# Attention: k and v in five slots with the rest rows, one reduction for k's maximum, the rest rows placed with the pair's second batch

## The chip, the cores and the metric
One Trainium2 chip, one core. The metric is the device time in microseconds (us) of one execution of the whole program: a linear attention over 8 batches and two mixture-of-experts layers behind it, in one launch.

## The reference
Shapes: q, k and v are [8 batches, 8 heads, 576 rows, 64]; x is 4608 tokens of 512; each of the two expert layers has 8 experts of 512 to 1024 to 512.

```
q_s = exp(q - max over d);    q_s /= sum over d
k_s = exp(k - max over rows); k_s /= sum over rows
kv  = k_s^T v                          # per head, 64 x 64
x   = q_s kv                           # to [4608, 512]
layer 1: tokens with x.w_skip > 0: x += gate * (relu(x w1[e]) w2[e]),  e = argmax(x w_gate)
layer 2: out = gate * (relu(x w1[e]) w2[e]),  e = argmax of the cosine of x and expert e, over tau
```

## The kernel before, in words
**Attention.** The 576 rows of a batch don't fill whole tiles of 128 partitions. The first 512 lie in four slots (partition p holds rows 4p to 4p+3, tiles `kt`, `vt`, `qt` of 128 x 8 heads x 4 slots x 64). The last 64, the rest rows, have tiles of their own (`kr`, `vr`, `qr`): the even batch of a pair has partitions 0 to 63 there, the odd batch 64 to 127. For each batch `do_k` finds the maximum of k over all rows, in two halves of four heads: VectorE takes pairwise maxima (L190 over slots 0,1 against 2,3; L191 over the two that are left; L192 with the rest rows, on 64 partitions), TensorE transposes (L194), VectorE reduces (L196), ScalarE spreads (L197), TensorE transposes back (L199), ScalarE copies to `mb` (L201). Then k minus the maximum is formed on GpSimd, in the batches of the parameter `kV` on VectorE (L203 for the slots, L205 or L206 for the rest rows), ScalarE takes the exponential (L207, L209) and copies v beside a column of ones (L208, L210). TensorE multiplies over the four slots (L219) and the rest rows (L220). `do_q` does the like for q (L255 to L262), on GpSimd except for the batches in `qV`. `do_out` transposes (L275), copies (L285), multiplies with kv and the router columns in one product (L290), and VectorE divides out of PSUM: L296, L297, L298 into `xb` (the token rows), L299 into `lp` (the logits by head). The rest rows of a pair go through as a slot of their own, into `xr` and `lr`.

**Placing.** `place` takes the slots of one batch (half a batch for the last two, the parameter `tail`; one slot for the rest rows of a pair: 14 calls in all) and finds each token's experts and its row in the DRAM table X: a sum over heads (L319), some ten small VectorE operations (L320 to L327, L338, L340, L341), three kinds of small products on TensorE (L330 to L332), two small copies on ScalarE (L342, L343), and for each slot one indirect DMA from GpSimd's queue (L348). L321 writes the shifted logits into the token rows in SBUF, L322 reads them there; the other intermediates lie in the SBUF tile `rt`, and the product's ranks in a PSUM tile `pr` from L330 to L340. `pr` is one of the four PSUM tiles `p1`, which the transposes and the products of k and v use too.

**The order.** All steps of attention are tasks with a due time (`step`, `off`, `ob` in `PRM`), a cost for each engine that can take them, and the tiles that they read and write. The planner `Order` makes the order of each engine's queue from these when the kernel is built: at each turn it takes, among the tasks that can start earliest, the one with the lowest due time. The engines run their queues in that order and wait for each other by semaphores. The tiles of a name are few (kt 2, vt 2, qt 2, xb 2, p1 4, po 2), and a task waits until one is free. SyncE issues the loads, in planned order too.

**Behind attention.** When the last `place` has the counts (`accF`), the first expert layer starts: the first 512 tokens of expert 0 are in the tile GE by then (L371, behind the placing of batch 6), its weights in the tiles of k and v (L358). L505 and L506 split weights into two parts on ScalarE, VectorE and GpSimd. Then both layers run in steps of 256 tokens. This code is the same before and after, up to a slice of the ring of token tiles.

Of the kernel before, what the change touches and what calls it, by code (L numbers as in the profile page):

```python
# [94 lines left out]
def attention(tc,nc,raw,ctx,cst,q,k,v,routers,wgt,enD,X,accF,w1,w2,early,prm={}):  # L95
# [68 lines left out]
    def load(t,src,b,prio,n,by):  # L164
        x=val((t+'t',b),t+'t',2); y=val((t+'r',b//2),t+'r',2)
        if t=='k': add(prio-.1,dict(D=.65),lambda e: nc.sync.dma_start(out=y.tile[half(b)],in_=rest(src,b)),writes=[(y,b%2)],lat=1.3,dma=.73)
        elif b%2==(t=='q'):
            add(prio+.1,dict(D=1.24),lambda e: [nc.sync.dma_start(out=y.tile[half(o)],in_=rest(src,b//2*2+o)) for o in range(2)],writes=[y],lat=1.3,dma=1.46)
        for g in range(n):
            def f(e,g=g):  # L170
                if by=='h': a=slice(H//n*g,H//n*g+H//n); nc.sync.dma_start(out=x.tile[:,a],in_=main(src,b)[:,a])
                else: nc.sync.dma_start(out=x.tile,in_=main(src,b))
            add(prio,dict(D=.48),f,writes=[x] if n==1 else [(x,g)],lat=1.25,dma=2.91/n)
        return x,y
    def pt(x,n,g): return [x] if n==1 else [(x,g)]
    def do_k(b):
        i=b//2; h=half(b); t0=b*step; n=fine.get(b,1); u=t0+at('k',b); NH=H//n; NC=4//n
        kt,kr=load('k',k,b,u-5,n,'h'); vt,vr=load('v',v,b,t0+at('v',b)-5,n,'h')
        m1=val(('m1',b),parts=2); m2=val(('m2',b),parts=2); m2b=val(('m2b',b),parts=2); mb=val(('mb',b),parts=2); ek=val(('ek',b),parts=2)
        vp=val(('vp',b),parts=2); vq=val(('vq',i),parts=2)  # L180
        fast=b in prm.get('kV',())

        ke=val(('ke',b),parts=2) if b%2 and not fast else None; kx=ke or kr
        for g in range(n):
            hs=slice(NH*g,NH*g+NH); cs=slice(NC*g,NC*g+NC); w=NC*128
# [11 lines left out]
            add(u+2,dict(A=.43/n+.09),lambda e,cs=cs: A.copy(m2b.tile[:,cs],m2.tile[:,cs].unsqueeze(2).to_broadcast([128,NC,128])),pt(m2,n,g),pt(m2b,n,g))  # L197
# [7 lines left out]
            if ke is None: add(u+3.4,sc,lambda e,hs=hs: E[e].tensor_tensor(out=kr.tile[h,hs],in0=kr.tile[h,hs],in1=mb.tile[h,hs],op=ALU.subtract),pt(mb,n,g),krp)  # L205
            else: add(u+3.4,sc,lambda e,hs=hs: E[e].tensor_tensor(out=ke.tile[:,hs],in0=kr.tile[:,hs],in1=mb.tile[:,hs],op=ALU.subtract),pt(mb,n,g)+[kr],pt(ke,n,g))  # L206
            add(u+4,dict(A=1.73/n+.07),lambda e,hs=hs: A.activation(out=ek.tile[:,:,hs],in_=ek.tile[:,:,hs],func=AF.Exp),[],pt(ek,n,g))  # L207
            add(t0+at('v',b),dict(A=1.73/n+.07),lambda e,hs=hs: A.copy(vp.tile[:,hs,:,0:D],vt.tile[:,hs]),pt(vt,n,g),pt(vp,n,g))  # L208
# [4 lines left out]
        for a in range(2):
            pk=val(('p1','kv',b,a)); ks=val(('ks',b,a)); p3=val(('p1','c',b,a)); p4=val(('p1','d',b,a))
            for c2 in range(2):
                c=2*a+c2
                def f(e,pk=pk,c=c,c2=c2):
                    o=pk.tile[:,130*c2:130*c2+130].rearrange("p (g w) -> p g w",g=2)
                    for j in range(NB): T.matmul(o,lhsT=ek.tile[:,j,2*c:2*c+2].rearrange(hd),rhs=vp.tile[:,2*c:2*c+2,j],start=j==0,stop=False)  # L219
                    T.matmul(o,lhsT=kx.tile[h,2*c:2*c+2].rearrange(hd),rhs=vq.tile[h,2*c:2*c+2],start=False,stop=True)  # L220
# [42 lines left out]
    def do_out(b):  # L263
# [3 lines left out]
        xb=val(('xb',b),parts=NB); lp=val(('lp',b),parts=NB); xr=val(('xr',i)); lr=val(('lr',i))  # L267
        order=list(range(NB+b%2))
        if b%2: order=[NB]+order[:-1]
        for z,j in enumerate(order):  # L270
            w=u+1.5*z; rem=j==NB
# [28 lines left out]
            if rem: place(('r',i),1,[xr],[lr],lambda: xr.tile.unsqueeze(1),lambda: lr.tile.unsqueeze(1),w+4,cst['ids'][:,4*B+i:4*B+i+1])  # L300
        ng=2 if b in tail else 1; NJ=NB//ng
        for g in range(ng):
            js=slice(NJ*g,NJ*g+NJ); parts=range(js.start,js.stop)
            place((b,g),NJ,[(xb,j) for j in parts],[(lp,j) for j in parts],lambda js=js: xb.tile[:,js],lambda js=js: lp.tile[:,js],at('S',b)-off['S']+(u+8 if ng==1 else u+1.5*(order.index(js.stop-1)+1)+1),cst['ids'][:,4*b+js.start:4*b+js.stop])
    units=[]; UE=prm.get('early',B-2)
    for b in range(B):
        if b%2: units.append(('r',b//2))
        units+=[(b,g) for g in range(2 if b in tail else 1)]
    def place(key,nj,xk,lk,xt,lt,prio,ids):
# [7 lines left out]
        def w(a,b): return rt.tile[:,0:nj,a:b]  # L317
# [3 lines left out]
        add(prio,dict(V=c),lambda e: V.tensor_tensor(out=xt()[:,:,512:528].rearrange("p j (g e) -> p j g e",g=2),in0=l2(),in1=w(16,18).unsqueeze(3).to_broadcast([128,nj,2,8]),op=ALU.subtract),[ls,rt],xk)  # L321
# [538 lines left out]
```

## Time and profile before

| | us |
|---|---|
| median of 3 runs | 1089.13 (1087.38 to 1093.6) |
| the profiled execution: device time / span | 1090.26 / 1088.5 |
| TensorE busy | 984.2 (90%) |
| VectorE busy | 632.7 (58%) |
| ScalarE busy | 466.7 (43%) |
| GpSimd busy | 413.9 (38%) |
| mean granted TensorE clock | 0.958 |

The page gives shares over the whole span; attention is its first 206 us. In the rows below PE is TensorE's matmul, PEld its weight load, DVE VectorE, ACT ScalarE, POOL GpSimd, SP SyncE. "<-" names what ended an idle time.

### The profile page before, as it was taken

The page shows a single profiled execution, that of the slowest core. Times are in us where ns is not written, and L with a number is a line of the kernel's source. Part 1 is how long each engine was busy: PE and PEld are TensorE (multiplying, and loading weights), DVE is VectorE, ACT ScalarE, POOL GpSimd, SP SyncE. Part 2 cuts the span into 40 slices and gives each one's busy share as a digit, 9 for nine tenths or more (in the row PEclk, how much of TensorE's full clock was granted, in tenths as well). Part 3 has the DMA queues.
Part 4 walks back from the last instruction along what each step waited for, and adds up shares of the span by engine and source line. Part 5 has one row for each costly group of instructions (what it writes and reads, how often), then busy time and mean ns, then how long its engine had stood idle before and what let it go on. Part 6 is the DMA issues. An engine that isn't in the chain of part 4 may idle for free. (4 is left out here: it accounts for less than half of the span.)

```text
span 1088.5 us, 19924 instructions
## 1 busy us (share of the span) xinstructions
PE 984.2 (90%) x6083; PEld 872.4 (80%) x6083; DVE 632.7 (58%) x1624; ACT 466.7 (43%) x971; POOL 413.9 (38%) x369
## 2 busy tenths in 40 slices
PE   3989689589789999999998899999999999999993
PEld 2868588478578988777997789988898899998892
DVE  4798888777546776675776533244443612265470
ACT  5757456412743326243223532262643531365351
POOL 6547544601793817438221730031221310043140
PEclk9988889789989999999999899999999999999998
DMA  9976543563353522425111156034160620062510
GB/s 282 301 231 216 170 156 119 202 217 121 119 205 102 181 76 82 157 88 196 48 42 44 50 192 232 21 121 146 31 231 21 231 71 21 21 212 82 185 38 22
DMA packets 84412, 143.72 MB, mean 132 GB/s; under 512 B 19215, under 2 KB 43791, under 8 KB 84064
## 3 DMA queue, kind: packets, MB, share of 16 engines
q1 hardware_dynamic: 74304, 114.37, 32.8%
q0 software_dynamic: 8640, 26.61, 6.4%
q8 instruction: 75, 1.23, 0.5%
q14 instruction: 145, 1.19, 0.4%
q10 hardware_dynamic: 1248, 0.32, 0.1%
HBM read 110.03 MB, written 33.68 MB: 132 GB/s over the span
## 5 line engine op out<-in xcount | busy, mean ns | idle before, releaser
L536 PE MATMUL P<-xT,w1h 128*128 128x256 f32 x1856 | 345.4, 288 | 5.1 <-ACTq L722 2.3
L566 PE MATMUL py<-w2h,hT 128*128 128x512 f32 x1072 | 343.6, 396 | 2.7 <-issue 2.4
L536 PEld LDWEIGHTS P<-xT,w1h 128*128 128x128 f32 x1856 | 298.3, 197 | 8.3 <-issue 3.6
L536 PE MATMUL P<-xT,w1l 128*128 128x256 f32 x928 | 267.9, 289 | 9.8 <-DVE w1l L506 5.3
L566 PEld LDWEIGHTS py<-w2h,hT 128*128 128x128 f32 x1072 | 201.6, 189 | 46.6 <-DVE hT L513 3.7
L566 PE MATMUL py<-w2l,hT 128*128 128x512 f32 x536 | 211.3, 394 | 4.4 <-POOL w2l L506 3.3
L540 DVE SCALAR_TENSOR_TENSOR hT<-P,hT 128x512 fp32r<-128x512 f32 x116 | 77.7, 687 | 213.4 <-ACT hT L539 204.3
L536 PEld LDWEIGHTS P<-xT,w1l 128*128 128x128 f32 x928 | 182.3, 196 | 11.6 <-POOL w1l L506 5.5
L638 DVE SCALAR_TENSOR_TENSOR jk<-py,enB 128x512 bf16<-128x512 f32 x198 | 136.9, 691 | 24.3 <-ACT xb L574 10.7
L578 POOL DMA_INDIRECT out_dram<-y,idt x38 | 38.2, 1006 | 287.5 <-ACT y L577 234.0
L539 ACT ACTIVATE hT<-P 128x512 fp32r<-128x512 f32 x116 | 68.0, 596 | 180.4 <-PE P L536 176.0
L566 PEld LDWEIGHTS py<-w2l,hT 128*128 128x128 f32 x536 | 101.2, 189 | 32.9 <-POOL w2l L506 10.3
L506 POOL TENSOR_TENSOR w1l<-kt,w1h 128x512 fp32r<-128x512 f32 x64 | 84.2, 1344 | 59.9 <-ACT w1h L505 51.8
L506 POOL TENSOR_TENSOR w2l<-vt,w2h 128x512 fp32r<-128x512 f32 x76 | 101.8, 1368 | 1.4 <-issue 0.8
L577 ACT ACTIVATE y<-py,gate 128x512 f32<-128x512 f32 x38 | 26.1, 688 | 117.6 <-PE py L566 110.9
L290 PE MATMUL po<-KV,eT 128*128 128x164 f32 x256 | 48.6, 342 | 11.7 <-DVE xr L298 9.0
L505 ACT CAST w2h<-vt 128x512 fp32r<-128x512 f32 x104 | 55.5, 617 | 6.4 <-issue 4.0
L505 ACT CAST w1h<-kt 128x512 fp32r<-128x512 f32 x104 | 55.6, 638 | 0.0
L290 PEld LDWEIGHTS po<-KV,eT 128*128 128x128 f32 x256 | 42.3, 216 | 13.4 <-DVE xr L298 9.5
L574 ACT COPY xb<-py 128x512 f32<-128x512 f32 x17 | 10.0, 587 | 96.9 <-DVE flag L649 50.6
L348 POOL DMA_INDIRECT X<-xb,pi x32 | 33.1, 1035 | 44.1 <-ACT pi L343 35.5
L513 DVE TENSOR_TENSOR hT<-P,hT 128x512 fp32r<-128x512 f32 x18 | 12.4, 687 | 63.8 <-ACT hT L512 63.8
(261 smaller groups left out, 1392.1 us busy)
## 6 DMA issues: line engine op xcount, KB each, us to landing
vt<-in_moe_w_dram SPq DMA_DIRECT2D x26, 1024.0 KB
kt<-in_moe_w_dram SPq DMA_DIRECT2D x26, 1024.0 KB
xb<-X SPq DMA_DIRECT2D x56, 266.0 KB
kt<-in_k_dram SPq DMA_DIRECT2D x16, 512.0 KB
vt<-in_v_dram SPq DMA_DIRECT2D x16, 512.0 KB
qt<-in_q_dram SPq DMA_DIRECT2D x8, 1024.0 KB
xg<-X SPq DMA_DIRECT2D x28, 266.0 KB
X<-empty SPq DMA_DIRECT2D x16, 266.0 KB
```

The source lines that it names most:

```text
L290: T.matmul(po.tile[:,c,0:CW],lhsT=eT.tile[:,c] if g is None else eT.tile[:,g,c],rhs=kv.tile[:,c],start=n==0,stop=n==len(ins)-1)
L348: i=P.indirect_dma_start(out=X,out_offset=IO(pi.tile[:,j:j+1]),in_=xt()[:,j],in_offset=None,bounds_check=ZROW,oob_is_err=False)
L505: nc.scalar.copy(h,a)
L506: (nc.gpsimd if lo[2*f+i]=='P' else nc.vector).tensor_tensor(out=l,in0=a,in1=h.bitcast(F32),op=ALU.subtract)
L513: self.nc.vector.tensor_tensor(out=l,in0=p,in1=h.bitcast(F32),op=ALU.subtract)
L536: T.matmul(o,lhsT=w[:,c,128*f:128*f+128],rhs=x[:,c],start=n==0,stop=n==11); n+=1
L539: A.activation(out=h,in_=q,func=AF.Relu)
L540: V.scalar_tensor_tensor(out=hl[:,f-1:f+1],in0=q,scalar=0.0,in1=h.bitcast(F32),op0=ALU.max,op1=ALU.subtract)
L566: T.matmul(self.py[t],lhsT=x[:,c,a],rhs=w[:,c],start=n==0,stop=n==23); n+=1
L577: A.activation(out=y,in_=p,func=AF.Copy,scale=gt)
L578: P.indirect_dma_start(out=self.out,out_offset=IO(self.idt[:,i:i+1]),in_=y,in_offset=None,bounds_check=NTOK-1,oob_is_err=False)
L638: for e in range(n) if 'V' in eng else (): self.nc.vector.scalar_tensor_tensor(out=self.jk,in0=self.py[t],scalar=1.0,in1=self.enB[:,e],op0 ...
```

## The change
- `kt`, `vt` get a fifth slot for the rest rows, as do `ek` (k's exponentials) and `vp` (v and ones). k's rest rows are loaded twice, into both halves of the partitions, in front of the main load; v's once, into partitions 0 to 63, and the other half of that slot is zero, with zeros in place of the ones. `kr`, `vr`, `vq`, `ke` are gone, with L192, L205, L206, L209, L210 and L220: one operation each now covers five slots, and the product runs over five slots of 128 partitions.
- k's maximum over the slots is one reduction per half (four heads x 64 columns x 5 slots, the slot as the innermost axis, 64 elements apart) in place of L190, L191 and L192.
- In the batches of `kV` the subtraction takes the maximum from PSUM; the copy to `mb` (L201) is left out there.
- The output of an odd batch has five slots in one tile `xb` (the pair's rest rows first). They are placed with that batch: 10 calls of `place` in place of 14. For the last batch the calls have three slots and two.
- In `place` the intermediates lie in the PSUM tile `pr`, which is taken at the first of them; ScalarE copies the shifted logits to the token rows at the end.
- The costs given to the planner and all its due times are new; `kV` is (1,6) for (3,7), `qV` (2,) for (7,), and `nA` (batches whose kv is scaled out of PSUM on ScalarE) (1,2,3,6,7) for (0,2,3,4,6,7).

```diff
-    mk('kt',[128,H,NB,D],nb['kt'],raw); mk('vt',[128,H,NB,D],nb['vt'],raw)
+    mk('kt',[128,H,NS,D],nb['kt'],raw); mk('vt',[128,H,NS,D],nb['vt'],raw)
...
+            add(prio-.1,dict(D=1.1),lambda e: [nc.sync.dma_start(out=x.tile[half(o),:,NB],in_=r) for o in range(2)],writes=[(x,2)],lat=1.3,dma=1.0)
+        else: add(prio-.1,dict(D=.6),lambda e: nc.sync.dma_start(out=x.tile[0:64,:,NB],in_=r),writes=[(x,2)],lat=1.3,dma=.5)
...
-            add(u,dict(V=1.07/n+.06),lambda e,hs=hs,t=t: V.tensor_tensor(out=t(),in0=kt.tile[:,hs,0:2],in1=kt.tile[:,hs,2:4],op=ALU.max),pt(kt,n,g),pt(ek,n,g))
-            add(u,dict(V=.54/n+.06),lambda e,hs=hs,t=t: V.tensor_tensor(out=m1.tile[:,hs],in0=t()[:,:,0],in1=t()[:,:,1],op=ALU.max),pt(ek,n,g),pt(m1,n,g))
-            add(u,dict(V=.54/n+.06),lambda e,hs=hs: V.tensor_tensor(out=m1.tile[h,hs],in0=m1.tile[h,hs],in1=kr.tile[h,hs],op=ALU.max),krp,pt(m1,n,g))
+            add(u,dict(V=1.40),lambda e,hs=hs: V.tensor_reduce(out=m1.tile[:,hs],in_=kt.tile[:,hs].rearrange("p h j d -> p h d j"),axis=AX.X,op=ALU.max),kp,pt(m1,n,g))
...
+            if fast:
+                add(u+3.5,dict(V=1.40),lambda e,hs=hs,p2=p2,w=w: V.tensor_tensor(out=ek.tile[:,:,hs].rearrange("p j h d -> p h j d"),in0=kt.tile[:,hs],in1=p2.tile[:,0:w].rearrange("p (h d) -> p h d",d=D).unsqueeze(2).to_broadcast([128,NH,NS,D]),op=ALU.subtract),kp+[p2],pt(ek,n,g))
...
-                    for j in range(NB): T.matmul(o,lhsT=ek.tile[:,j,2*c:2*c+2].rearrange(hd),rhs=vp.tile[:,2*c:2*c+2,j],start=j==0,stop=False)
-                    T.matmul(o,lhsT=kx.tile[h,2*c:2*c+2].rearrange(hd),rhs=vq.tile[h,2*c:2*c+2],start=False,stop=True)
+                    for j in range(NS): T.matmul(o,lhsT=ek.tile[:,j,2*c:2*c+2].rearrange(hd),rhs=vp.tile[:,2*c:2*c+2,j],start=j==0,stop=j==NB)
...
-            if rem: place(('r',i),1,[xr],[lr],lambda: xr.tile.unsqueeze(1),lambda: lr.tile.unsqueeze(1),w+4,cst['ids'][:,4*B+i:4*B+i+1])
-        ng=2 if b in tail else 1; NJ=NB//ng
+        ng=2 if b in tail else 1; cut=[0,ns] if ng==1 else [0,ns-2,ns]
...
-        def w(a,b): return rt.tile[:,0:nj,a:b]
+        def w(a,b): return pr.tile[:,96:96+36*NS].rearrange("p (j c) -> p j c",c=36)[:,0:nj,a:b]
+        def sh(): return pr.tile[:,288:288+16*NS].rearrange("p (j c) -> p j c",c=16)[:,0:nj]
+        rt=pr
...
-        add(prio,dict(V=c),lambda e: V.tensor_tensor(out=xt()[:,:,512:528].rearrange("p j (g e) -> p j g e",g=2),in0=l2(),in1=w(16,18).unsqueeze(3).to_broadcast([128,nj,2,8]),op=ALU.subtract),[ls,rt],xk)
+        add(prio,dict(V=c),lambda e: V.tensor_tensor(out=sh().rearrange("p j (g e) -> p j g e",g=2),in0=l2(),in1=w(16,18).unsqueeze(3).to_broadcast([128,nj,2,8]),op=ALU.subtract),[ls],[rt])
...
+        add(prio+.3,dict(A=.22),lambda e: A.copy(xt()[:,:,512:528],sh()),[pr],xk)
```

## Rows read from the trace of the kernel before

**Rows 1.** Busy time by stretch: us, then busy us (instructions) by engine, clock, DMA share, GB/s.
```profile
0.00:206.00 206.00, 156.64 (x1015) 138.42 (x1016) 166.35 (x449) 116.81 (x258) 109.85 (x118) 0.90 0.68 208
...
40.00:190.00 150.00, 126.15 (x833) 114.20 (x833) 133.64 (x345) 90.40 (x204) 78.58 (x58) 0.87 0.59 190
...
8.00:40.00 32.00, 22.14 (x127) 17.35 (x127) 20.14 (x34) 20.80 (x40) 18.32 (x14) 1.00 1.15 316
```

**Rows 2.** Timeline of GpSimd, VectorE and TensorE: start, us, engine, line, instruction.
```profile
104.28 9.25 DVE L321 TENSOR_TENSOR xb<-ls,rt 128x64 f32<-128x64 f32 x1
...
108.82 4.63 POOL L203 TENSOR_TENSOR ek<-kt,mb 128x1024 f32<-128x1024 f32 x2
...
114.53 2.56 PE L290 MATMUL po<-KV,eT 128*128 128x164 f32 x8 [7.08 <-DVE xr L298]
...
154.17 1.28 PE L290 MATMUL po<-KV,eT 128*128 128x164 f32 x8
```

**Rows 3.** VectorE's groups by shape, 0 to 206 us: busy us, mean ns, idle before.
```profile
L191 DVE TENSOR_TENSOR m<-ek 128x256 f32<-128x256 f32 x16 | 15.7, 991 | 0.1
...
L190 DVE TENSOR_TENSOR ek<-kt 128x512 f32<-128x512 f32 x16 | 14.4, 905 | 0.0
...
L321 DVE TENSOR_TENSOR xb<-ls,rt 128x64 f32<-128x64 f32 x6 | 14.2, 2372 | 0.0
...
L192 DVE TENSOR_TENSOR m<-m,kr 64x256 f32<-64x256 f32 x16 | 10.6, 675 | 0.2
...
L205 DVE TENSOR_TENSOR kr<-kr,mb 64x256 f32<-64x256 f32 x4 | 6.0, 1498 | 0.1
...
L203 DVE TENSOR_TENSOR ek<-kt,mb 128x1024 f32<-128x1024 f32 x4 | 4.9, 1224 | 0.1
...
L327 DVE TENSOR_TENSOR oh<-desc,rt 128x16 bf16<-128x16 f32 x4 | 4.0, 994 | 0.0
```

**Rows 4.** Shortest, median and longest duration in ns of single lines, 0 to 206 us.
```profile
L191 DVE TENSOR_TENSOR m<-ek x16: 373/416/5658, 9.2 to 148.2; 128x256 f32<-128x256 f32 x16
...
L321 DVE TENSOR_TENSOR xb<-ls,rt x10: 181/206/9251, 56.9 to 203.2; 128x64 f32<-128x64 f32 x6, 128x32 f32<-128x32 f32 x4
...
L298 DVE TENSOR_TENSOR xb<-po,rc x32: 671/681/695, 42.0 to 201.7; 128x512 f32<-128x512 f32 x32
```

**Rows 5.** VectorE's reductions and small groups by shape, same view and stretch as Rows 3.
```profile
L255 DVE TENSOR_REDUCE qx<-qt 128x16 f32<-128x1024 f32 x16 | 19.1, 1206 | 0.0
...
L319 DVE TENSOR_REDUCE ls<-lp 128x68 f32<-128x544 f32 x6 | 6.5, 1080 | 0.0
...
L319 DVE TENSOR_REDUCE ls<-lr 128x17 f32<-128x136 f32 x4 | 1.4, 361 | 0.0
...
L341 DVE TENSOR_REDUCE pf<-rt 128x1 f32<-128x16 f32 x4 | 0.7, 163 | 0.0
...
L340 DVE TENSOR_TENSOR rt<-p,oh 128x64 f32<-128x64 f32 x6 | 1.3, 215 | 0.0
...
L231 DVE TENSOR_TENSOR KV<-p,ks 64x128 f32<-64x128 f32 x8 | 2.2, 280 | 0.2
```

**Rows 6.** Seven stretches at half clock, the fourth and their sum; columns as in Rows 1.
```profile
112.00:118.50 6.50, 3.98 (x19) 3.62 (x20) 6.46 (x21) 1.31 (x5) 1.44 (x1) 0.50 0.57 163
...
sum 35.00, PE 27.76 PEld 25.54 DVE 30.62 ACT 12.84 POOL 11.72; mean PE 3.97 PEld 3.65 DVE 4.37 ACT 1.83 POOL 1.67
```

**Rows 7.** Timeline at the end of attention.
```profile
198.59 0.88 SPq L371 DMA_DIRECT2D GE<-X  x2
...
205.59 1.09 PE L525 MATMUL pxT<-ident,GE 128*128 128x128 f32 x4 [0.39 <-DVE rt L340]
```

**Rows 8.** Timeline: a transposition that waits for one of the four PSUM tiles.
```profile
144.30 0.66 PE L275 MATMUL p<-ident,eq 128*128 128x128 f32 x4 [2.29 <-DVE rt L340]
```

**Rows 9.** GpSimd's groups, 0 to 206 us, columns as in Rows 3.
```profile
L348 POOL DMA_INDIRECT X<-xb,pi x30 | 31.2, 1039 | 43.5 <-ACT pi L343 35.5 <-issue 6.3 <-ACT xb L342 1.2
...
L203 POOL TENSOR_TENSOR ek<-kt,mb 128x1024 f32<-128x1024 f32 x12 | 28.1, 2348 | 0.0
```

More of the change, by code (lines that the diff above doesn't have):

```diff
@@ L163, in attention, with load, loadq @@
     add=sch.add
[L164 to L173, printed above, removed]
+    def load(t,src,b,prio):
+        x=val((t+'t',b),t+'t',3); r=rest(src,b)
+        if t=='k':
+            add(prio-.1,dict(D=1.1),lambda e: [nc.sync.dma_start(out=x.tile[half(o),:,NB],in_=r) for o in range(2)],writes=[(x,2)],lat=1.3,dma=1.0)
+        else: add(prio-.1,dict(D=.6),lambda e: nc.sync.dma_start(out=x.tile[0:64,:,NB],in_=r),writes=[(x,2)],lat=1.3,dma=.5)
+        for g in range(2):
+            a=slice(H//2*g,H//2*g+H//2)
+            add(prio,dict(D=.48),lambda e,a=a: nc.sync.dma_start(out=x.tile[:,a,0:NB],in_=main(src,b)[:,a]),writes=[(x,g)],lat=1.25,dma=1.45)
+        return x
+    def loadq(b,prio):
+        x=val(('qt',b),'qt',2); y=val(('qr',b//2),'qr',2)
+        if b%2: add(prio+.1,dict(D=1.24),lambda e: [nc.sync.dma_start(out=y.tile[half(o)],in_=rest(q,b//2*2+o)) for o in range(2)],writes=[y],lat=1.3,dma=1.46)
+        add(prio,dict(D=.48),lambda e: nc.sync.dma_start(out=x.tile,in_=main(q,b)),writes=[x],lat=1.25,dma=2.91)
         return x,y
@@ L176, in do_k @@
     def do_k(b):
-        i=b//2; h=half(b); t0=b*step; n=fine.get(b,1); u=t0+at('k',b); NH=H//n; NC=4//n
-        kt,kr=load('k',k,b,u-5,n,'h'); vt,vr=load('v',v,b,t0+at('v',b)-5,n,'h')
+        t0=b*step; n=2; u=t0+at('k',b); NH=H//n; NC=4//n
+        kt=load('k',k,b,u-5); vt=load('v',v,b,t0+at('v',b)-5)
         m1=val(('m1',b),parts=2); m2=val(('m2',b),parts=2); m2b=val(('m2b',b),parts=2); mb=val(('mb',b),parts=2); ek=val(('ek',b),parts=2)
-        vp=val(('vp',b),parts=2); vq=val(('vq',i),parts=2)
+        vp=val(('vp',b),parts=2)
         fast=b in prm.get('kV',())
-        ke=val(('ke',b),parts=2) if b%2 and not fast else None; kx=ke or kr
         for g in range(n):
@@ L196, in do_k @@
             add(u+1.5,dict(V=.53/n+.07),lambda e,p=p,cs=cs,w=w: V.tensor_reduce(out=m2.tile[:,cs],in_=p.tile[:,0:w].rearrange("p (c w) -> p c w",c=NC),axis=AX.X,op=ALU.max),[p],pt(m2,n,g))
-            add(u+2,dict(A=.43/n+.09),lambda e,cs=cs: A.copy(m2b.tile[:,cs],m2.tile[:,cs].unsqueeze(2).to_broadcast([128,NC,128])),pt(m2,n,g),pt(m2b,n,g))
+            add(u+2,dict(A=.40),lambda e,cs=cs: A.copy(m2b.tile[:,cs],m2.tile[:,cs].unsqueeze(2).to_broadcast([128,NC,128])),pt(m2,n,g),pt(m2b,n,g))
             def f(e,p2=p2,g=g):
@@ L205, in do_k @@
[L205 to L208, printed above, removed]
@@ L212, in do_k @@
+            add(u+4,dict(A=1.28),lambda e,hs=hs: A.activation(out=ek.tile[:,:,hs],in_=ek.tile[:,:,hs],func=AF.Exp),[],pt(ek,n,g))
+            add(t0+at('v',b),dict(A=1.28),lambda e,hs=hs: A.copy(vp.tile[:,hs,:,0:D],vt.tile[:,hs]),[(vt,g),(vt,2)],pt(vp,n,g))
         KV=val(('KV',b),parts=2); u=t0+at('K',b); kT=val(('kT',b),parts=2)
@@ L249, in do_q @@
         i=b//2; t0=b*step; n=fine.get(b,1); u=t0+at('q',b); NJ=NB//n
-        qt,qr=load('q',q,b,u-5,1,'j')
+        qt,qr=loadq(b,u-5)
         fast=b in prm.get('qV',())
@@ L266, in do_out @@
         KV=val(('KV',b),parts=2); eq=val(('eq',b),parts=2); qr=val(('qr',i),'qr',2)
[L267 to L271, printed above, removed]
+        xb=val(('xb',b),parts=NS); lp=val(('lp',b),parts=NS); s0=b%2; ns=NB+s0
+        for z in range(ns):
+            w=u+1.5*z; j=z-s0; rem=j<0
             pq=val(('p1','q',b,j)); po=val(('po',b,j)); rc=val(('rc',b,j))
@@ L299, in do_out @@
             add(w+1,dict(V=.21),lambda e,po=po,rc=rc,lo=lo: V.tensor_tensor(out=lo().rearrange("p (c g) n -> p c g n",g=2),in0=po.tile[:,:,130:164].rearrange("p c (g n) -> p c g n",g=2),in1=rc.tile.unsqueeze(3).to_broadcast([128,4,2,17]),op=ALU.mult),[po,rc],lk)
-            if rem: place(('r',i),1,[xr],[lr],lambda: xr.tile.unsqueeze(1),lambda: lr.tile.unsqueeze(1),w+4,cst['ids'][:,4*B+i:4*B+i+1])
-        ng=2 if b in tail else 1; NJ=NB//ng
+        ng=2 if b in tail else 1; cut=[0,ns] if ng==1 else [0,ns-2,ns]
         for g in range(ng):
-            js=slice(NJ*g,NJ*g+NJ); parts=range(js.start,js.stop)
-            place((b,g),NJ,[(xb,j) for j in parts],[(lp,j) for j in parts],lambda js=js: xb.tile[:,js],lambda js=js: lp.tile[:,js],at('S',b)-off['S']+(u+8 if ng==1 else u+1.5*(order.index(js.stop-1)+1)+1),cst['ids'][:,4*b+js.start:4*b+js.stop])
+            sl=slice(cut[g],cut[g+1]); parts=range(sl.start,sl.stop); nj=len(parts); i0=9*i+4*s0
+            place((b,g),nj,[(xb,z) for z in parts],[(lp,z) for z in parts],lambda sl=sl: xb.tile[:,sl],lambda sl=sl: lp.tile[:,sl],at('S',b)-off['S']+(u+8 if ng==1 else u+1.5*sl.stop+1),cst['ids'][:,i0+sl.start:i0+sl.stop])
     units=[]; UE=prm.get('early',B-2)
     for b in range(B):
-        if b%2: units.append(('r',b//2))
         units+=[(b,g) for g in range(2 if b in tail else 1)]
@@ L328, in f @@
         def f(e):
-            o=pr.tile[:,0:64].rearrange("p (j c) -> p j c",c=16); h=oh.tile
+            o=pr.tile[:,0:16*NS].rearrange("p (j c) -> p j c",c=16); h=oh.tile
             T.matmul(o[:,0:nj],lhsT=cst['tri'],rhs=h[:,1:1+nj],start=True,stop=False)
@@ L480, in __init__ @@
         self.xT=st("xT",[128,4,256],F32R,2); self.hT=st("hT",[128,8,256],F32R,2)
-        self.ring=list(ring)+st('xg',[128,4,XW]); self.h,=st("h",[128,1024])
+        self.ring=[t[:,0:4] for t in ring]+st('xg',[128,4,XW]); self.h,=st("h",[128,1024])
         self.ys=st("y",[128,512],n=2)
```

71 lines of the change are left out of this document (34 added, 37 removed).

## The prediction
> **What bounds the kernel now.** I read the busy time by stretch first. Everything that the change touches ends at about 206 us; of the 1088.5 us span the other 883 run code that stays as it is, so the gain or loss is what the end of attention moves. In those 206 us VectorE counts 166.35 us busy, TensorE 156.64, ScalarE 116.81, GpSimd 109.85 [rows 1]. Between 40 and 190 us VectorE is busy 133.64 of 150: by that count it is the bound.
>
> The timeline then says what that busy time is made of. L321, 128x64 elements, lasts 9.25 us from 104.28, to 113.53; GpSimd's last subtraction in a run without a pause ends at 113.45 (108.82 + 4.63); TensorE waits 7.08 us for L298, which stands behind L321 on VectorE [rows 2]. The same line has a median of 206 ns [rows 4]. L191 goes from 373 to 5658 ns, while L298, more than twice as long at the median, stays between 671 and 695 in 32 cases [rows 4]. What separates them is where the inputs lie: L298 reads one input from SBUF and one from PSUM, L191 and L321 read both from SBUF. So I read the long ones as waits for GpSimd inside VectorE, which befall only instructions with two SBUF inputs.
>
> Two groups show the size [rows 3]. L321 costs 14.2 us for six, 13.0 more than six times its median 206 ns [rows 3, 4]; four one-slot L327 cost 4.0, of which 3.3 are wait if one takes as long as the one-slot L341, 163 ns [rows 3, 5]. With the stretched ones of L190, L191, L192 and L205 I estimate some 37 us of wait in VectorE's 166.
>
> [...]
>
> **VectorE, part by part.** From 166.35 us:
> - k's maximum: L190, L191 and L192 go, 14.4 + 15.7 + 10.6 = 40.7 [rows 3]. Sixteen reductions of 1280 elements come. Their price has two rows. L255, whose innermost axis is contiguous, does 1024 in 1206 ns; at its 1.04 ns each beyond the fixed part (an estimate, from 1206 and a fixed part near 0.14 us) 1280 take 1.47 us. L319, whose innermost axis is strided, goes from 361 ns for 136 to 1080 for 544, 1.76 ns each [rows 5]; 1280 take 1080 + 736 x 1.76 = 2.38 us. The new operation strides (64 elements), so I take L319's: 16 x 2.38 = 38.0. The lower end is 23.5. [...]
> - The new reduction has one SBUF input, like L255 and L319, and by the reading above it doesn't wait. Neither do L203 (its maximum now in PSUM) or the small operations of `place` (one side in PSUM).
> - L321: -13.0, the wait alone.
> - The four placements of rest rows go: ten one-slot groups from L319 (1.4) to L341 (0.7), 11.0 together with L327's wait [rows 3, 5]. A slot more in four placements brings them back in part: 136 x 1.76 ns = 0.24 for L319 and an estimated 0.02 for each of some nine others (L340 at four slots 215, L341 at one 163 ns), so 4 x 0.4 = +1.6.
> - L205 and L203, 10.9 together [rows 3], become four of 1280 elements: 4 x 1.224 x 1.25 = 6.1, so -4.8.
> - One batch more scales kv on VectorE: four L231 of 0.28 [rows 5] and four small copies, +2.
> - Small operations through PSUM: L340, which reads PSUM, lasts 215 ns against L321's median of 206 [rows 4, 5]; +0.6 for some 70 of them. [...]
> - Two L256 in batch 2 still have two SBUF inputs: each can wait from nothing to 9.25 us; I take 2 for both.
>
> Sum: 166.35 - 40.7 + 38.0 - 13.0 - 11.0 + 1.6 - 4.8 + 2 + 0.6 + 2 = 141. VectorE's share of the 206 us was 0.81; at that share 141 us end at 174.6. VectorE alone would allow a gain of 31.
>
> **TensorE is next late.** Its products stay (L220 becomes a fifth slot of L219). If half of the 27.76 us at half clock goes, as eight L290 at 1.28 for 2.56 say, once the long waits are gone, 156.64 becomes 142.8. At its present share, 0.76, that ends at 187.8 us: a gain of 18.2. This is the smaller of the two, and I take it. Bounds: no clock gained, and TensorE's share unchanged, gives nothing; a share of 0.84 as between 40 and 190 us (126.15 of 150) [rows 1] gives 170 and a gain of 36.
>
> **What hides and what doesn't.**
> - GpSimd: 1280 elements in one subtraction cost at most 2.35 x 1.25 = 2.94 [rows 9], 0.6 more than the four slots, and the rest rows' own subtraction goes; twelve of them, at most 7 us, lie beside 96 us of idle [rows 1]; nothing.
> - ScalarE: ten copies of the logits, at most 0.2 each like the other small ones, beside 89 us of idle; nothing, but up to 0.2 in front of the last scatter.
> - Loads: k's rest rows twice, 8 x 0.13 MB more. At 316 GB/s in 8 to 40 us, where the queue's share is 1.15 [rows 1], each is 0.4 us; four fall there, 1.7 us at most, the others are hidden (share 0.59 later). These loads stand in front of the main loads on SyncE's queue. I take +1.
> - The last batch: its rest rows are now scattered with the first three slots, so five scatters stand after the last counts instead of four. At 1.04 us and a pause of 0.3 [rows 9] GpSimd is free for L506 1.3 us later: +1.3. If it is hidden, 0.
> - GE is issued at 198.59, seven us ahead of its first use, which waits for L340, not for it [rows 7]. It covers what the tail may shrink by some 3 us (estimate: 1.06 MB at 316 GB/s is 3.4); beyond that GE is late.
>
> Net gain 18.2 - 1 - 1.3 = 16. The profiled execution took 1090.26, so 1074.3; the median of the runs shown is 1.1 lower. Predicted: **1073**.
>
> **The rivals.**
> - *TensorE closes up (0.16).* With VectorE at 141 or less, TensorE reaches a share of 0.80: 142.8/0.80 = 178.5, a gain of 27.5, less 2.3: 1064. For it: 0.84 was reached between 40 and 190 us, waits included. Against: two engines at nearly the same load, each queue in a fixed order.
> - *The gain is lost in the order (0.11).* TensorE and ScalarE waited for other things that the waits covered; the clock still falls. A third of the gain, 5 us: 1084. For it: new due times for every task, written by a planner that counts 1.40 for the maximum where I count 2.38. Against: TensorE's own waits named a stretched VectorE instruction or one behind it [rows 2].
> - *A PSUM tile is held too long (0.12), slower.* `place` now takes one of four `p1` tiles at its first small operation rather than at L330, and keeps it until ScalarE's copy. The trace has the wait once: at 144.30 transpositions stand 2.29 us for L340, which frees such a tile [rows 8]. At 2.3 us for each of ten placements 23 us are lost against 16 gained: 1097 - 1 = 1096. It decides from 1.6 us per placement on. Against: three tiles are left, and the planner knows of the hold.
> - *The change does not do what it says (0.06).* If instructions with one SBUF input waited too, the 37 us would stay elsewhere, and the strided reductions would eat what the placements give: about 1090. Against: L298's 671 to 695 ns in 32 cases [rows 4].
> - The reduction turns the result only if it costs over 3.2 us (141 + 16 x 0.8 = 153 is TensorE's 187.8 at 0.81); over 4 us it makes the kernel slower. No row is that dear per element.
>
> **How the numbers follow.** The forecast has 0.55, with its own range 1066 to 1080. A change under 0.5% (5.4 us) can't be told from none. Faster: 0.55 + 0.16 + half of 0.11 = 0.76. Same: the other half and 0.06 = 0.12. Slower: 0.12. The range 1057 to 1088 goes down to a share of 0.84 for TensorE (less what the loads and the scatters take back) and up to where nearly all is lost; about 0.15 stands above, 0.04 below.
>
> **What would show it.** Right: attention's end near 190 us; no small VectorE instruction over 1 us beside GpSimd except L256; the reduction of k's maximum near 2.4 us (1.5 would say that the stride costs nothing there); VectorE near 141 us busy; fewer stretches at clock 0.50. Wrong: the first product of the expert layer at 200 us or later; TensorE waiting for a `p1` tile that a placement holds; small VectorE operations that still end when a GpSimd operation ends.

## The result, and the profile after

| | before | after |
|---|---|---|
| median of 4 runs each, same chip, us | 1091.37 (1087.38 to 1093.87) | 1057.47 (1056.23 to 1061.93) |
| the profiled execution: device time / span, us | 1090.26 / 1088.5 | 1061.93 / 1060.1 |
| attention's end in it, us | 205.6 | 176.3 |

The ratio is 0.9712, 95% interval 0.9677 to 0.9747: 31 us of 1089 where 16 were forecast (the two medians above differ by 33.9). On a second chip the same two kernels gave 0.9682 (0.9642 to 0.9723). What follows attention took 882.9 us before (1088.5 - 205.6) and 883.8 after: the whole gain lies in attention. The profiled execution after is the slowest of its four, 4.5 us above their median.

Busy time of the kernel after by stretch, columns as in [rows 1]; below it the five stretches at half clock that fall in attention (the last is cut at its end) as one sum, which answers to [rows 6].

```profile
0.00:176.30 176.30, 136.85 (x1005) 125.41 (x1005) 147.45 (x376) 112.19 (x232) 106.92 (x111) 0.95 0.79 246
40.00:160.00 120.00, 103.97 (x779) 97.39 (x779) 105.79 (x275) 81.96 (x178) 75.32 (x47) 0.94 0.75 239
8.00:40.00 32.00, 22.50 (x148) 18.91 (x148) 27.55 (x40) 21.99 (x31) 17.32 (x21) 1.00 1.13 330
...
sum 16.60, PE 14.01 PEld 13.79 DVE 10.99 ACT 12.59 POOL 8.97; mean PE 2.80 PEld 2.76 DVE 2.20 ACT 2.52 POOL 1.79
```

VectorE fell by 18.7 us (166.14 to 147.45 at attention's end), TensorE by 19.4, and the end by 29.3. So 10.6 us more went than VectorE worked less.

VectorE's groups by shape in the first 176 us, columns as in [rows 3]: the reduction in place of L190 to L192, the divisions, the subtraction of the batches in `kV` and of q, and an example of the small operations of `place`.

```profile
L191 DVE TENSOR_REDUCE m<-kt 128x256 f32<-128x1280 f32 x16 | 37.9, 2383 | 0.1
L292 DVE TENSOR_TENSOR xb<-po,rc 128x512 f32<-128x512 f32 x36 | 24.3, 678 | 0.1
...
L202 DVE TENSOR_TENSOR ek<-kt,p 128x1280 f32<-128x1280 f32 x4 | 5.9, 1478 | 1.0 <-PE p L198 1.0
L252 DVE TENSOR_TENSOR eq<-qt,qx 128x1024 f32<-128x1024 f32 x2 | 4.8, 2381 | 0.0
...
L316 DVE TENSOR_TENSOR p<-ls,p 128x80 f32<-128x80 f32 x3 | 0.7, 238 | 0.0
```

Shortest, median and longest duration of two of them, as in [rows 4]. L316 is L321 of before, which went up to 9251 ns: it now stays under 250. Of the shapes that run more than once only L252 is stretched (3560 ns where the other one took 1202); it is the only one of them that still reads two inputs from SBUF.

```profile
L191 DVE TENSOR_REDUCE m<-kt x16: 2284/2384/2447, 8.9 to 125.2; 128x256 f32<-128x1280 f32 x16
...
L316 DVE TENSOR_TENSOR p<-ls,p x10: 185/218/246, 48.2 to 173.8; 128x64 f32<-128x64 f32 x3, 128x80 f32<-128x80 f32 x3, 128x32 f32<-128x32 f32 x3, 128x48 f32<-128x48 f32 x1
```

What TensorE waited for in the first 160 us of the kernel after (the waits of the page's trace: engine and line, its releaser; us in total, times, longest). The 8.2 us lie at the start, ahead of the first batch. The largest after that is VectorE's reduction; the entries that name an operation of `place` on its PSUM tile come to 4.6 us in all (L316 2.8, L318 1.2, L336 0.6).

```profile
PE p L193 <- DVE m L191: 11.4, 8, 2.5
PE p L150 <- DVE lp L147: 8.2, 1, 8.2
PE p L216 <- DVE p L316: 2.8, 1, 2.8
PE po L285 <- DVE xb L292: 2.7, 2, 2.0
```

TensorE's products of k with v, columns as in [rows 3]: first three rows of the kernel before, up to 205.6 us, then the one row of the kernel after that takes their place, up to 176.3 us.

```profile
L219 PE MATMUL p<-vp,ek 128*128 128x130 f32 x256 | 40.4, 307 | 0.3 <-ACT vp L208 0.3
L220 PE MATMUL p<-vq,kr 64*128 64x130 f32 x48 | 12.6, 346 | 1.9 <-ACT kr L209 1.9
L220 PE MATMUL p<-vq,ke 64*128 64x130 f32 x16 | 4.1, 340 | 0.0
...
L216 PE MATMUL p<-vp,ek 128*128 128x130 f32 x320 | 43.7, 290 | 3.7 <-DVE p L316 2.8 <-DVE m L195 0.4 <-ACT ek L206 0.4
```

The timeline at the end of attention, which answers to [rows 7]: GE is issued 4.1 us ahead of its first use (7.0 before), the last of five scatters ends at 180.24, and behind it lies a long instruction of VectorE, L504. L510's idle time is put down to GE's load, but it is the time of the transpositions just before it (1.12 us, begun without a wait for GE): in the second profile of this kernel the same 1.14 us name them, PE pxT L523.

```profile
172.30 0.88 SPq L367 DMA_DIRECT2D GE<-X  x2
...
176.36 1.12 PE L523 MATMUL pxT<-ident,GE 128*128 128x128 f32 x4 [0.79 <-ACT xb L339]
...
177.56 0.58 ACT L510 CAST xT<-pxT 128x512 fp32r<-128x512 f32 x1 [1.14 <-DMA GE<-X]
...
179.26 0.98 POOL L344 DMA_INDIRECT X<-xb,pi  x1 [0.30 <-issue]
...
180.48 5.01 POOL L504 TENSOR_TENSOR w1l<-kt,w1h 128x512 fp32r<-128x512 f32 x4
...
182.18 8.75 DVE L504 TENSOR_TENSOR w1l<-kt,w1h 128x512 fp32r<-128x512 f32 x1
...
190.98 0.58 PE L534 MATMUL P<-xT,w1l 128*128 128x256 f32 x1 [6.05 <-DVE w1l L504]
```

The kernel before has the same wait there: its L506 took 8.73 us from 211.38.

### The profile page after: what moved, and what is told of

Its sections match the earlier page's. It is cut to its first block, busy times and chain, and to the rows that moved or that the text cites. A ratio compares the mean times of both kernels' runs of the same rounds, so it can differ in the third digit from the quotient of the medians.

```text
span 1060.1 us, 19802 instructions
## 1 busy us (share of the span) xinstructions
PE 966.6 (91%) x6075; PEld 861.2 (81%) x6075; DVE 612.7 (58%) x1552; ACT 462.0 (44%) x945; POOL 410.3 (39%) x363
## 5 line engine op out<-in xcount | busy, mean ns | idle before, releaser
L504 POOL TENSOR_TENSOR w1l<-kt,w1h 128x512 fp32r<-128x512 f32 x64 | 83.8, 1340 | 59.7 <-ACT w1h L503 51.5
L504 POOL TENSOR_TENSOR w2l<-vt,w2h 128x512 fp32r<-128x512 f32 x76 | 101.2, 1360 | 1.4 <-ACT w2h L503 0.8
L344 POOL DMA_INDIRECT X<-xb,pi x36 | 36.2, 1007 | 33.5 <-ACT pi L338 12.4
L635 POOL TENSOR_TENSOR pr<-xb,enB 128x512 f32<-128x512 f32 x20 | 25.4, 1291 | 60.0 <-ACT xb L572 60.0
L546 PE MATMUL P<-w1h,xT 128*128 128x512 f32 x144 | 47.4, 401 | 0.0
```

The source lines that it names most:

```text
L344: i=P.indirect_dma_start(out=X,out_offset=IO(pi.tile[:,j:j+1]),in_=xt()[:,j],in_offset=None,bounds_check=ZROW,oob_is_err=False)
L504: (nc.gpsimd if lo[2*f+i]=='P' else nc.vector).tensor_tensor(out=l,in0=a,in1=h.bitcast(F32),op=ALU.subtract)
L546: T.matmul(self.P4[f],lhsT=x[:,c,0:128],rhs=w[:,c,512*f:512*f+512],start=n==0,stop=n==11); n+=1
L635: for e in range(n,8) if 'P' in eng else (): self.nc.gpsimd.tensor_tensor(out=self.pr[e-n],in0=x,in1=self.enB[:,e],op=ALU.mult)
```

## The experiments

Theory ("waits"): VectorE sets attention's end; instructions with two SBUF inputs wait for GpSimd inside VectorE, and the change takes such inputs away. Rivals: the new due times bring the gain ("order"), or TensorE is the next limit, as the prediction took it. Ratios are to the kernel before on the same chip. A single profile can be some us off: two of the kernel after ended attention at 176.3 and 167.6.

**1. The new code under the old due times.** Only `PRM` is the old one (due times, `kV`, `qV`, `nA`).

```diff
-PRM={... 'step': 10.171, ... 'kV': (1, 6), 'qV': (2,), 'nA': (1, 2, 3, 6, 7), 'off': {'k': -11.99, ...
+PRM={... 'step': 10.1768, ... 'kV': (3, 7), 'qV': (7,), 'nA': (0, 2, 3, 4, 6, 7), 'off': {'k': -6.4845, ...
```

> The changed kernel with the due times and lists (kV, qV, nA) of the kernel before. Theory 'waits': the gain comes from VectorE's instructions no longer waiting for GpSimd, so nearly all of it stays: 1058 to 1068 us. Rival 'order': the gain comes from the new due times, so most of it goes: 1075 to 1092 us.

1070.18 us, ratio 0.9833 (0.9778 to 0.9888). The busy time until attention's end:

```profile
0.00:185.50 185.50, 141.08 (x1005) 130.14 (x1005) 144.27 (x368) 115.40 (x244) 106.24 (x110) 0.92 0.74 235
```

Both have a part: the code brings 18 us (1.67% of 1087), what is in `PRM` some 13 of the 31 (each of the two ratios is known to about half a hundredth, some 6 us).

**2. The intermediates of `place` back in SBUF**, order kept, so that its small operations have two SBUF inputs again.

```diff
-        def w(a,b): return pr.tile[:,96:96+36*NS]...
+        def w(a,b): return RT[n%2][:,0:36*NS]...   # two tiles rtx in SBUF; sh() likewise
```

> The changed kernel, every engine's order kept, with the intermediates of place in SBUF instead of PSUM, so that L316, L317 and L321 have two SBUF inputs again. 'Waits': these small operations last until GpSimd's run ends, 8 to 16 us of wait return on VectorE and the end comes 6 to 14 us later: 1064 to 1072 us. 'Order' or 'TensorE sets the end': within 3 us of the changed kernel, 1055 to 1061 us.

1064.25 us, 0.9794 (0.9736 to 0.9851): about half of what separates the kernel after from experiment 6 comes back. First the busy time until attention's end, then the stretched groups by shape.

```profile
0.00:182.40 182.40, 138.62 (x1005) 128.02 (x1006) 158.03 (x377) 112.77 (x232) 106.72 (x111) 0.93 0.75 238
```
```profile
L317 DVE TENSOR_TENSOR rtx<-ls,rtx 128x80 f32<-128x80 f32 x3 | 5.5, 1835 | 0.0
L318 DVE SCALAR_TENSOR_TENSOR rtx<-rtx,desc 128x80 f32<-128x80 f32 x3 | 3.3, 1099 | 0.0
L323 DVE TENSOR_TENSOR oh<-desc,rtx 128x64 bf16<-128x64 f32 x3 | 2.8, 926 | 0.0
```

The same 128x80 subtraction that took 238 ns takes 1835: 'waits' holds for the placing.

**3. k's maximum as three pairwise maxima**, order kept.

```diff
-  V.tensor_reduce(out=m1.tile[:,hs],in_=kt.tile[:,hs].rearrange("p h j d -> p h d j"),axis=AX.X,op=ALU.max)
+  V.tensor_tensor(out=t2,in0=kt.tile[:,hs,0:2],in1=kt.tile[:,hs,2:4],op=ALU.max)
+  V.tensor_tensor(out=m1.tile[:,hs],in0=t2[:,:,0],in1=t2[:,:,1],op=ALU.max)
+  V.tensor_tensor(out=m1.tile[:,hs],in0=m1.tile[:,hs],in1=kt.tile[:,hs,NB],op=ALU.max)
```

> The changed kernel, every engine's order kept, with k's maximum by three operations with two SBUF inputs (0.68 + 0.41 + 0.41 us undisturbed) in place of the reduction of 2.38 us. Without waits VectorE would have 14 us less to do. 'Waits': some 16 us of waiting for GpSimd come back and eat it, 1055 to 1066 us. Rival (the waits were no matter, VectorE's work is): 1043 to 1050 us.

1064.39 us, 0.9773 (0.9714 to 0.9833), attention's end 179.9 with VectorE 153.0 busy. The groups by shape:

```profile
L193 DVE TENSOR_TENSOR t2x<-kt 128x512 f32<-128x512 f32 x16 | 17.4, 1086 | 0.1
L194 DVE TENSOR_TENSOR m<-t2x 128x256 f32<-128x256 f32 x16 | 16.8, 1050 | 0.6
L195 DVE TENSOR_TENSOR m<-m,kt 128x256 f32<-128x256 f32 x16 | 9.4, 585 | 0.5
```

2.72 us per half for 2.38 in one reduction: the reduction is dear, and still cheaper than three that wait.

**4. The same reduction over contiguous elements.**

```diff
-  out=m1.tile[:,hs], in_=kt.tile[:,hs].rearrange("p h j d -> p h d j")
+  out=m1.tile[:,hs].rearrange(hd), in_=kt.tile[:,hs].rearrange("p h j d -> p (h j d)").rearrange("p (x j) -> p x j",j=NS)
```

> The changed kernel, every engine's order kept, with the reduction of k's maximum reading its 1280 elements contiguously, five neighbours at a time (each column is then shifted by another value than its maximum). 'The stride costs': 1.47 us instead of 2.38, VectorE has 14.6 us less. If VectorE sets the end of attention: 12 to 17 us faster, 1041 to 1046 us. If TensorE is next late, as the prediction had it: at most 5 us faster, 1052 to 1058 us. If the stride costs nothing: the duration stays at 2.38 us.

1042.23 us, 0.9586 (0.9531 to 0.9642). The busy time until attention's end, and two groups:

```profile
0.00:159.60 159.60, 131.57 (x1006) 121.64 (x1006) 132.87 (x377) 111.99 (x232) 106.88 (x111) 0.99 0.86 272
```
```profile
L191 DVE TENSOR_REDUCE m<-kt 128x256 f32<-128x1280 f32 x16 | 23.3, 1471 | 0.1
L251 DVE TENSOR_REDUCE qx<-qt 128x16 f32<-128x1024 f32 x16 | 19.3, 1208 | 4.7 <-DMA qt<-in_q_dram 4.6
```

14.6 us less of VectorE make the ratio 0.0111 smaller than the mean of the kernel after, 0.9697, which is 12 us: in the range of the theory. VectorE sets the end of the kernel after, and TensorE, at a share of 0.82 now, does not close it. What begins to be late is a load of q (4.6 us).

**5. The first split of weights:** all of w1 on VectorE, all of w2 on GpSimd (before: both on both).

```diff
-  self.split(0,(...))    ...    self.split(1)
+  self.split(0,(...),'V'*8)    ...    self.split(1,(),'P'*8)
```

> The changed kernel with the first split of weights behind attention shared out otherwise: w1's eight parts all on VectorE, w2's all on GpSimd (in the changed kernel they alternate; there one VectorE part waits 8.75 us behind GpSimd's run and TensorE 6.05 us for it). 'Two SBUF inputs wait for GpSimd': VectorE's parts of w1 run at 0.67 us each before GpSimd begins, TensorE's wait goes, 4 to 7 us faster than the changed kernel. Rival (the share of work matters, not the wait): no change within 2 us, or slower, since GpSimd's eight take 10 us.

1042.04 us, 0.9604 (0.9561 to 0.9647), 9.8 us under the kernel after on the same chip (1051.86), more than expected. Timelines: first the kernel after on that chip, then this one.

```profile
171.76 5.01 POOL L504 TENSOR_TENSOR w1l<-kt,w1h 128x512 fp32r<-128x512 f32 x4
173.47 8.73 DVE L504 TENSOR_TENSOR w1l<-kt,w1h 128x512 fp32r<-128x512 f32 x1
...
182.25 0.58 PE L534 MATMUL P<-xT,w1l 128*128 128x256 f32 x1 [5.58 <-DVE w1l L504]
```
```profile
173.99 1.27 DVE L504 TENSOR_TENSOR w1l<-kt,w1h 128x512 fp32r<-128x512 f32 x2
174.93 12.06 POOL L504 TENSOR_TENSOR w2l<-vt,w2h 128x512 fp32r<-128x512 f32 x8 [2.72 <-ACT w2h L503]
176.71 6.64 DVE L504 TENSOR_TENSOR w1l<-kt,w1h 128x512 fp32r<-128x512 f32 x4
...
183.40 0.38 PE L534 MATMUL P<-xT,w1l 128*128 128x256 f32 x1 [0.27 <-DVE w1l L504]
```

Of VectorE's first four parts, 1.27 us for two, three end before GpSimd's late start and the fourth 0.33 us behind it. The last four run beside it and are stretched still, 6.64 us for four, but none lasts as long as GpSimd's run, and GpSimd's eight need 12.06 us for 9.93 before. Attention ended at 167.6 in both. TensorE waits 5.3 us less for L504 and, over the whole execution, is 4.7 us less busy (960.9 to 956.2, with a granted clock of 0.92 for 0.86 in the 52 us behind attention); that is 10.0 of the 11.1 us between the two profiles. This wait lies outside the change, and the same reading finds it.

**6. Both waits back** (2 and 3 together, order kept).

> The kernel after with both sources of the wait for GpSimd back, its order kept: the intermediates of the placing in SBUF, and k's maximum as three pairwise maxima with two SBUF inputs. Alone the first cost 1.1 points of the ratio and the second 0.9. Theory 'VectorE's busy time sets the end, and the waits add': VectorE some 163 us busy until attention's end near 187, ratio 0.986 to 0.993. Rival 'the waits cover each other' (GpSimd's runs are the same, and one stretched instruction absorbs what two would have waited): VectorE 155 to 160, end 180 to 184, ratio 0.977 to 0.984.

1074.65 us, 0.9918 (0.9892 to 0.9943).

```profile
0.00:190.70 190.70, 142.10 (x1005) 132.47 (x1006) 162.03 (x409) 113.28 (x231) 107.99 (x111) 0.89 0.72 228
```

The waits add: alone 1.0 and 0.8 points (hundredths of the ratio) over the kernel after (0.9697, the mean of its two ratios), together 2.2; that they cover each other is ruled out, that they add exactly is not shown, at half a point of noise in each. The clock fell with them, from 0.95 and 0.98 to 0.89.

**7. The kernel before with the placing in PSUM alone**, the hold of a `p1` tile and ScalarE's copy included.

```diff
-        def w(a,b): return rt.tile[:,0:nj,a:b]
+        def w(a,b): return pr.tile[:,96:96+36*NB]...    # sh() and A.copy(xt()[:,:,512:528],sh()) as in the change
```

> The kernel before with one part of the change alone: the intermediates of place in PSUM, with the copy by ScalarE. 'Waits': L321's and L327's 16 us of wait go, 8 to 16 us faster than before: 0.985 to 0.993. Rival 'a PSUM tile held too long': TensorE's transpositions wait for a p1 tile that a placement holds, at 2.3 us for each of fourteen placements it is not faster, 0.998 to 1.02.

1074.84 us, 0.9899 (0.9836 to 0.9962), attention's end 191.2. The hold costs nothing that outweighs the wait: the rival of the PSUM tile falls.

```profile
0.00:191.20 191.20, 151.48 (x1013) 132.51 (x1013) 152.89 (x449) 117.74 (x272) 107.44 (x118) 0.94 0.73 224
```

**8. One maximum per head, spread by ScalarE.**

```diff
+  V.tensor_reduce(out=mh.tile[:,hs],in_=kt.tile[:,hs].rearrange("p h j d -> p h (j d)"),axis=AX.X,op=ALU.max)
+  A.copy(m1.tile[:,hs],mh.tile[:,hs].unsqueeze(2).to_broadcast([128,NH,D]))
```

> The changed kernel with one maximum for each head (over its rows and its 64 columns, 320 contiguous elements a partition) in place of one for each column; ScalarE spreads it. The shift of k is then at least each column's maximum. VectorE's reduction is contiguous: 1.5 us instead of 2.38, 14 us less in all; ScalarE gets 16 copies of 0.4 and each half's chain a step more, and the planner moves some tasks. 'VectorE sets the end': 8 to 16 us faster than the changed kernel. 'The chain through the maximum sets it': no gain, or slower.

1048.33 us, 0.9655 (0.9616 to 0.9694): 3.5 us under the kernel after on its chip, less than expected.

```profile
L192 DVE TENSOR_REDUCE mh<-kt 128x4 f32<-128x1280 f32 x16 | 23.5, 1479 | 1.7 <-DMA kt<-in_k_dram 1.6
L253 DVE TENSOR_REDUCE qx<-qt 128x16 f32<-128x1024 f32 x16 | 19.3, 1211 | 5.2 <-DMA qt<-in_q_dram 5.1
```

The reduction is as cheap as in 4, but VectorE stands idle 32.0 us (131.6 busy, end 163.6) where 4 has 26.7. The step on ScalarE lengthens the chain and changes the order; which of the two costs it was not separated.

**9. The contiguous maximum under the old due times** (1 and 4 together).

> The contiguous maximum (again another value than the column's maximum) under the due times of the kernel before, the order of which is that of the run with the old due times (ratio 0.9833, attention's end 185.5). Theory 'VectorE sets the end in either order': 14.6 us of busy time less, at least 10 of them seen at the end: ratio 0.968 to 0.975, end 171 to 176. Rival 'in the old order TensorE and the order set the end' (what the prediction took for the change as a whole): 0 to 5 us, ratio 0.978 to 0.985, end 180 to 186, with VectorE's idle time grown by what it no longer works.

1056.15 us, 0.977 (0.9731 to 0.981): between the two ranges, and its interval meets that of 1. The trace decides more:

```profile
0.00:168.40 168.40, 135.93 (x1005) 126.00 (x1005) 129.53 (x368) 114.67 (x244) 106.50 (x110) 0.95 0.82 259
```

In the same order as 1, VectorE works 14.7 us less, its idle time did not grow (41.2 to 38.9), and TensorE's share rose from 0.76 to 0.81. So TensorE had waited for VectorE in the old order too. How much the end moves is less sure: the traces have 17 us between the two ends, but one is of the slowest execution of 1, the other of the fastest of 9, and the ratios differ by 0.0063, some 7 us.

**10. 4 and 5 together.**

> The kernel after with two edits: the reduction reads its five neighbours from contiguous addresses (what is subtracted from a column of k is then another value than that column's maximum, as in the run of the contiguous maximum), and the first split gives all of w1 to VectorE and all of w2 to GpSimd. Alone the first gave 0.9586 and the second 9.8 us. Theory 'two separate places' (VectorE's busy time sets the end of attention; behind it TensorE waits for the slowest of the first split): the gains add, ratio to the kernel before 0.947 to 0.955, attention's end near 160 and no wait for L504 over 1 us. Rival 'the loads close in' (with attention shorter the weights and GE land late and the first product waits for them): ratio 0.956 to 0.962, and the first products of the expert layer wait for a transfer.

1034.25 us, 0.9566 (0.953 to 0.9602). The ratio lies in the rival's range, but what the rival rests on, a wait for a transfer, isn't there. Against 0.9586 of 4 the split can't be told from nothing by ratio. In the traces attention ends at 158.0 (159.6 in 4), TensorE's wait for VectorE's L504 falls from 5.2 to 0.8 us, the rest after attention from 878.9 to 872.8 us, and no first product waits for a transfer. So the wait goes as in 5; the 6 us behind attention are not a measure of it, since with the old split that stretch took anything from 878.7 (2) to 885.9 us (1).

**11. 8 and 5 together.**

> One maximum per head over its 320 contiguous elements, spread by ScalarE (what is subtracted is the head's maximum, not the column's), and the first split with all of w1 on VectorE and all of w2 on GpSimd. Alone the first gave 0.9655 and the second 9.8 us on its chip. Theory 'two separate places': ratio 0.954 to 0.960. Rival 'the longer chain with ScalarE's step is late at the end, and the split hides behind it': ratio 0.961 to 0.967.

1042.53 us, 0.9637 (0.96 to 0.9674): the rival's range. Behind attention (161.2 to 1040.1) 878.9 us, in 8 882.7: the wait of 5.8 us for VectorE's part of w1 is gone, but 3.8 us are inside the spread named in 10. Why the split's 9.8 us don't come back here stays open.

## Why the prediction was right and where it failed

The direction was right, the size was half. The measured 1057.47 us lies at the lowest edge of the range, 1057 to 1088, and the second chip's 1051.86 below it. That edge was to be reached by a TensorE share of 0.84; the share was 0.78 (136.85 of 176.3). That the number still falls into the range is luck.

Attention's end less VectorE's busy time until then, in us, from the rows above and the profiles of each kernel:

| order | kernel | VectorE | end | rest |
|---|---|---|---|---|
| old | before | 166.1 | 205.6 | 39.5 |
| old | before, placing in PSUM (7) | 152.9 | 191.2 | 38.3 |
| old | new code (1) | 144.3 | 185.5 | 41.2 |
| old | new code, contiguous maximum (9) | 129.5 | 168.4 | 38.9 |
| new | both waits back (6) | 162.0 | 190.7 | 28.7 |
| new | placing in SBUF (2) | 158.0 | 182.4 | 24.4 |
| new | pairwise maxima (3) | 153.0 | 179.9 | 26.9 |
| new | after, two profiles | 147.5, 147.1 | 176.3, 167.6 | 28.9, 20.5 |
| new | contiguous maximum (4) | 132.9 | 159.6 | 26.7 |

Each row is one profile. Experiment 5, whose attention is that of the kernel after, gave 147.1, 167.6 and 20.5 like the second of its two profiles; 10, with the maximum of 4, gave 132.8, 158.0 and 25.2. So a single end is known to some 8 us. Within an order the end follows VectorE's busy time about one for one, over 37 us in the old and 29 in the new. The rest belongs to the order: 39.5 and 26 on the mean (20.5 to 28.9).

- *What bounds the kernel, and the waits:* right. With two inputs in SBUF the 128x80 subtraction of the placing took 1835 and 2271 ns on the mean (2, 6), with one in PSUM 238 in the kernel after; the 128x64 one of the kernel before went from 2372 ns [rows 3] to 214 (7). The pairwise maxima of 3 took 1086, 1050 and 585 ns, where L190, L191 and L192 have medians of 680, 416 and 420. So the rival that the change doesn't do what it says falls, too. By what mechanism the two engines get in each other's way was not shown.
- *The reduction:* 2.38 us taken, 2383 ns measured; 1.47 as the lower end, 1471 measured in 4 with contiguous elements. L319's price was the right one of the two; why the stride costs it was not shown. The other price fits 4 as well: 1471 ns for 1280 contiguous elements and 1208 for L251's 1024 are 1.03 ns each beyond 0.15 us, where 1.04 and 0.14 were estimated.
- *The sum of 141:* each term was right. The durations of all VectorE instructions up to attention's end add up to 194.2 us before and 168.3 after, 25.9 less, where the terms of the sum had 25.4. But VectorE's busy time fell only 18.7. The 448 instructions before overlap by 28 us in all, 63 ns each; taking away 72 short ones takes away little more than what sticks out. The sum took durations from a busy time in which the overlaps count once: 141 was to be 147.
- *"TensorE is next late":* the step that failed. It held TensorE's share, 0.76, for a property of TensorE. It was VectorE's doing: with VectorE alone made cheaper the share went to 0.81 in the same order (1 to 9), 0.82 in the new one (4; 0.78 and 0.79 in the two profiles of the kernel after). Its sign, an end of attention near 190 us, didn't come: 176.3 and 167.6. That experiment 1 ended at 185.5 with TensorE at 141.1, beside the forecast 187.8 and 142.8, doesn't save the step: 147 + 39.5 is 187 as well.
- *The order:* costed at nothing in the sum, and as a loss in a rival. `PRM` brought about 13 of the 31 us (1); which of due times, `kV`, `qV` and `nA` did it was not tried. The planner's 1.40 for an operation of 2.38 did not spoil it.
- *TensorE's 142.8:* the term let the time at half clock run at full clock, 13.9 us less, and let the products stay. TensorE's busy time fell by 19.4, and neither part was right. The seven stretches of [rows 6] leave one out, at 146 us (first row below); all eight together have TensorE busy for 33.63 us (the sum below). Of these 14.01 are left, and the 19.6 that went are worth some 10 at full clock (an estimate, from the two times of eight L290 in [rows 2], 2.56 and 1.28 us). And the products didn't stay: those of k with v took 57.1 us (40.4 + 12.6 + 4.1) and take 43.7, 13.4 less; one product of 128x130 went from 307 to 290 ns on the mean, at a granted clock of 0.90 and 0.95. That the time at half clock goes with the long waits was the author's estimate: no run has this part alone, but the end doesn't follow it: from 7 to 1 TensorE's busy time fell by 10.4 us, VectorE's by 8.6 and the end by 5.7, and in 2, 3, 4 and 9 the end moved while TensorE's products stayed.

```profile
146.06:149.47 3.41, 3.41 (x17) 3.37 (x16) 3.27 (x12) 2.21 (x4) 2.50 (x4) 0.50 0.41 162
sum 42.47, PE 33.63 PEld 31.36 DVE 37.82 ACT 17.35 POOL 15.20; mean PE 4.20 PEld 3.92 DVE 4.73 ACT 2.17 POOL 1.90
```

- *The PSUM tile:* no (7), and TensorE's list of waits after names placing operations on such a tile with 4.6 us in all, where 23 were feared.
- *Beside other work:* GpSimd's subtraction of 1280 takes 2910 ns (at most 2.94 was said) and costs nothing to be seen; q's two L252 cost 2.4 us over two unstretched ones (2 said). From GE's issue to its first use 2.9 us went, about the 3 that the prediction said it covers, and neither profile of the kernel after shows it late. The 1.3 us for the last scatters can't be told in 882.9 against 883.8.

## What to carry to other kernels

Where VectorE and GpSimd work side by side, compare the longest duration of an instruction with its median (9251 and 206 ns for L321 [rows 4]): a VectorE instruction with two SBUF inputs may be waiting inside its busy time, and here one input in PSUM ended that (1835 ns in 2, 238 in the kernel after, for the same subtraction). Before calling another engine the next limit because of its busy share, see whom its waits name; if they name the engine that you are relieving, the share can rise, as TensorE's did here from 0.76 to 0.81 (1 to 9). Subtract from an engine's busy time only what its instructions hold alone, not their durations: VectorE's durations fell by 25.9 us here, its busy time by 18.7.

## What the runs showed that was not expected

- 1280 fp32 elements in groups of five: 2383 ns with 256 bytes between neighbours, 1471 ns contiguous, for the same instruction and count.
- Neighbouring VectorE instructions overlap in the records, by 63 ns an instruction on the mean in the kernel before and 55 after: the sum of durations is 17% and 14% above the busy time.
- One VectorE subtraction of 128x512 (0.67 us otherwise) took 8.75 us and ended 0.56 us behind the last of eight of GpSimd's (5.01 us for four, 4.92 for four). In experiment 5 four such subtractions took 1.66 us each on the mean beside eight of GpSimd's, which were stretched too, 12.06 us for 9.93. What decides between the two no run shows.
- The kernel after ended attention at 176.3 us in one profile and at 167.6 in another, with VectorE's busy time within 0.4 us (on a second chip, where experiment 5 has 167.6 too; whether chip or execution makes it is not shown): the idle time differs, 28.9 and 20.5, and so does the granted clock, 0.95 and 0.98.
